# A quarter of the gate section of `w_mod` is loaded early into 16 partitions

## The chip, the cores and the metric

The kernel runs on one core of one Trainium2 chip. The metric is the device time of one execution in microseconds (us). Engines are named as in the profile: PE (TensorE matmul), PEld (TensorE weight load), DVE (VectorE), ACT (ScalarE), POOL (GpSimd), SP (SyncE, which here only issues DMAs). "bufA", "bufB" and "bufC" appear in the profile as bA, bB and bC.

## The reference

One decode step of a block with adaptive layer norm: batch 4, one token each, width 512; attention with 32 heads over a cache of 4096 keys and values of width 128, then a gated MLP. All tensors are bfloat16.

```python
mod = (silu(c) @ w_mod).reshape(4, 6, 1, 512)      # sa, ca, ga, sb, cb, gb
h = layernorm(x) * (1 + ca) + sa
q = h @ wq                                          # 512 -> 32 heads x 128
p = softmax(q @ k_cache^T * 128**-0.5)              # 4 x 32 x 4096 keys
x = x + ga * ((p @ v_cache) @ wo)
h = layernorm(x) * (1 + cb) + sb
z = gelu(h @ w_in); z1, z2 = z[:, :896], layernorm(z[:, 896:])
x = x + gb * ((z1 * (w_sp * z2 + b_sp)) @ w_out)
```

The caches are 2 x 134 MB; everything else together is about 15 MB. `w_mod` has 512 rows of 6 x 512 columns; its last 512 columns make `gb`, the gate of the second half. This is the "gate section", 512 KB.

## The kernel before

Three buffers of 64 KB per partition hold what is loaded. Keys alternate between bufA and bufB, values go to bufC. A "pair" is one load of 8 MB: eight heads of one batch row, 64 KB in each of 128 partitions. `load_k(i)` and `load_v(i)` issue the loads; the loop `for i in range(NT)` has 32 steps of four heads: the first 30 are halves of 15 pairs, the last two (N0 and L) have loads of their own of 4 MB.

All big loads are issued by SP, in program order, so they form one stream: `wq` (4 MB) and the first five sections of `w_mod` (2.5 MB) into bufC, the first key pair in two halves (`load_k(0)`, two issues of L143), the second key pair (`load_k(2)`, L143), and then in the loop values and keys in turn. SP waits for the buffer's last reader before it issues a load into it. ACT issues four tiny loads: `c` and `x` at the very beginning, `w_sp` and `b_sp` (L347, L348) after the queries. The schedule is manual: each engine runs its instructions in the order in which the source records them, and an engine that waits holds up all that stands behind it.

The beginning, in the source's order: `c` is turned by four transposes (`rows_to_cols`), goes through the sigmoid into `cT`, and `mod_rows(0, 2)` (L273) multiplies it with two sections of `w_mod` as rows; ACT copies them to `mrows` (L278), and `mod_turn(2)` (L283) transposes them back to columns. Then come the queries (L323 to L341), `mod_rows(2, 3)` for three more sections, and the loop. In step 0, after the two multiplications of keys (L381) and the first reduction on PE (L389), `late_mod_b` turns the three sections into `modT`, and broadcasts `w_sp` and `b_sp` by a matmul (L356). The first value load may only be issued when all of this has been read, since it overwrites bufC.

In a step, DVE multiplies keys by the query (L381), PE sums over the width with an identity matmul (L389), DVE sums the rest (L401, L412), ACT takes exponentials (L455), and PE multiplies with the values (L510).

The end: `load_end` (called in step L) issues `wo`'s last part (L591, two loads), `w_in` (L594, two), `w_out` (L596, two) and the gate section as `wg_sb` (L601) in four loads of 128 KB, one for each of the four rows that a partition holds. After the last values the chain runs through the projection (L671), the layer norm, the MLP (L836), its normalisation (L220 with `inv_f`), the output product `y` (L862), and `gb` from `wg_sb` and `cT` (L870, 16 matmuls, four for each of the four loads). DVE combines `y` (L890 to L901), multiplies with `gb` (L902), PE transposes (L904), DVE adds `x` (L906) and SP stores (L907).

Of the kernel before, what the change touches and what calls it, by code (L numbers as in the profile page):

```python
# [8 lines left out]
BF16 = mybir.dt.bfloat16  # L9
F32 = mybir.dt.float32  # L10
# [8 lines left out]
RD = 8  # L19
TAIL = (64, 32, 16, 16)  # L20
KIN = (slice(0, 2), slice(2, 4))
KG = tuple(slice(k, k + 1) for k in range(4))
JW = (slice(0, 4), slice(4, 7))
RW = (slice(0, 4), slice(4, 8))

# [26 lines left out]
def kernel(  # L52
# [16 lines left out]
    nc = tc.nc  # L69
    P = 128  # L70
    B, _, D = A_x.shape
    _, H, SK, DH = A_k_cache.shape
    F = B_w_in.shape[1]
    FH = F // 2
    DJ = D // P
# [4 lines left out]
    R = P // HQ  # L80
# [15 lines left out]
    ident_bf = front.tile([P, P], BF16, name="ident_bf")  # L96
# [27 lines left out]
    wm = w_mod.rearrange("(p j) n -> p j n", p=P)  # L124
# [21 lines left out]
    def load_k(i):  # L146
        if i < N0:
            load(bufs[i // 2 % 2], kv_view(A_k_cache, i), (NJ, NJ) if i == 0 else (NP,))
        else:
            load(kts[i], kv_view(A_k_cache, i), (NJ,))  # L150
# [5 lines left out]
            load(vts[i], kv_view(A_v_cache, i), TAIL if i == L else (NJ,))  # L156

    load_k(0)
    load_k(2)

    make_identity(nc, ident_bf)
    ident_f = consts.tile([P, P], F32, name="ident_f")
# [16 lines left out]
    def spread(n, pattern, axis, **sizes):  # L179
# [18 lines left out]
        out=far, in0=half, scalar1=-1.0, scalar2=-NEG, op0=ALU.add, op1=ALU.mult  # L198
# [1 line left out]
    nc.gpsimd.tensor_scalar(  # L200
        out=fars, in0=far[:, :, None].to_broadcast([P, 2, R // 2]), scalar1=-1.0, scalar2=None, op0=ALU.mult
    )
    cT = consts.tile([P, DJ, B], BF16, name="cT")
    pbd8 = consts.tile([P, NP, HP], BF16, name="pbd")
    nc.gpsimd.memset(pbd8, 0.0)
    pbds = pbd8.rearrange("p n q -> p (n q)").rearrange("p (k n q) -> p k n q", k=4, q=HQ)
# [5 lines left out]
    def rows_to_cols(src):  # L212
        t = ps_sm([P, DJ, B], BF16)
        for j in range(DJ):
            nc.tensor.transpose(t[:, j, :], src[0:B, j:D:DJ], ident_bf[0:B, 0:B])
        return t
# [34 lines left out]
        rsqrt(rs, v, 1.0, eps)  # L251
        return xc, rs

    cps = rows_to_cols(c_sb)
    cx = pre.tile([P, DJ, B], F32, name="cx")
    nc.vector.tensor_copy(out=cx, in_=cps)
    sg = pre.tile([P, DJ, B], F32, name="sg")
    nc.vector.tensor_scalar(
        out=sg, in0=cx, scalar1=-60.0, scalar2=-1.0, op0=ALU.max, op1=ALU.mult
    )  # L260
# [19 lines left out]
    def mod_turn(n):  # L280
        mps = ps_sm([P, DJ, n * R])
        for j in range(DJ):
            nc.tensor.transpose(mps[:, j, :], mrows[0:n * R, j:D:DJ], ident_f[0:n * R, 0:n * R])  # L283
        return mps.rearrange("p j (s r) -> p s j r", s=n)[:, :, :, 0:B]
# [6 lines left out]
    nc.vector.tensor_tensor(out=xn, in0=xc1, in1=bc(rs1, DJ), op=ALU.mult)  # L291
    mod_rows(0, 2)
    modA = mod_turn(2)
    hs = pre.tile([P, DJ, B], F32, name="hs")
    nc.vector.scalar_tensor_tensor(  # L295
        out=hs, in0=modA[:, 1], scalar=1.0, in1=xn, op0=ALU.add, op1=ALU.mult
# [49 lines left out]
    sp_t = pre.tile([1, 2], BF16, name="sp_t")  # L346
    nc.scalar.dma_start(out=sp_t[:, 0:1], in_=B_w_sp[0:1, 0:1])  # L347
    nc.scalar.dma_start(out=sp_t[:, 1:2], in_=B_b_sp.rearrange("(a b) -> a b", b=1))  # L348
    modT = consts.tile([P, 3 * DJ, B], F32, name="modT")
    g8 = consts.tile([P, 2, B], F32, name="g8")  # L350
    spf = consts.tile([P, 2], F32, name="spf")

    def late_mod_b():
        mps = mod_turn(3)
        sps = ps_sm([P, 2])
        nc.tensor.matmul(sps, lhsT=ones_b, rhs=sp_t, start=True, stop=True)  # L356
        nc.vector.tensor_copy(
            out=modT.rearrange("p (s j) b -> p s j b", s=3),
            in_=mps,
        )  # L360
        nc.vector.tensor_copy(out=spf, in_=sps)
        nc.gpsimd.tensor_copy(out=g8[:, 1, :], in_=spf[:, 0:1].to_broadcast([P, B]))
        cbT = modT[:, 2 * DJ:3 * DJ, :]
        nc.gpsimd.tensor_scalar_add(out=cbT, in0=cbT, scalar1=1.0)
# [210 lines left out]
    wol_sb = Arena(bufC, 0, 8 * KB).tile([P, HP, D], BF16)  # L575
    win_sb = Arena(bufC, 8 * KB, 22 * KB).tile([P, DJ, F], BF16)
    wout_sb = Arena(bufC, 22 * KB, 29 * KB).tile([P, NH, D], BF16)
    wg_sb = Arena(bufC, 29 * KB, 33 * KB).tile([P, DJ, D], BF16)
    tl = Arena(bufC, 33 * KB, 64 * KB)
    NL = GP * HP * DH  # L580

# [6 lines left out]
    def load_end():  # L588
        wol = A_wo[NL:H * DH].rearrange("(p r) n -> p r n", p=P)
        for rs in RW:  # L590
            nc.sync.dma_start(out=wol_sb[:, rs], in_=wol[:, rs])  # L591
        win = B_w_in.rearrange("(p j) n -> p j n", p=P)
        for ks in KIN:
            nc.sync.dma_start(out=win_sb[:, ks], in_=win[:, ks])  # L594
        for js in JW:
            nc.sync.dma_start(  # L596
                out=wout_sb[:, js],
                in_=B_w_out[js.start * P:js.stop * P].rearrange("(p j) n -> p j n", p=P),
            )
        for ks in KG:  # L600
            nc.sync.dma_start(out=wg_sb[:, ks], in_=wm[:, ks, 5 * D:])  # L601

    acc = late.tile([P, DJ, B], F32, name="acc")
    st2 = late.tile([P, 2, B, DJ + 1], F32, name="st2")
# [75 lines left out]
    for i in range(NT):  # L680
        mult(i, 0)
        if i >= 1:
            scores(i - 1)
        for k in normed_in(i - 1):
            norm_b(k)
        pick = i - 3 if i % 2 == 0 and i >= 4 else None
        if i % 2 and 3 <= i < L:
            pv(i - 2)
        if i % 2 and i < N0:
            load_v(i)  # L690
        reduce_d(i, 0)
        if pick:
            o_pick(pick)
            o_cols(pick)
        if i == L - 1:
            deal(0)
        if i == L:
            deal(2)
            pv(N0 - 1)
            load_end()  # L700
            nc.gpsimd.memset(pbd8, 0.0)  # L701
            nc.vector.memset(opss[1], 0.0)
            exps(N0)
        mult(i, 1)
        if i == 0:
            late_mod_b()
        for k in normed_in(i):
            norm_r(k)
        if pick:
            o_scale(pick)  # L710
        sum8(i, 0)
        if i == L - 1:
            dealt(0)
        if i == L:
            dealt(1)
            dealt(2)
            o_pick(N0 - 1)
            nc.vector.memset(opss[0], 0.0)
        reduce_d(i, 1)
        sum_rest(i)  # L720
        for k in normed_in(i):
            norm_a(k)
        if i == L - 1:
            deal(1)
        if i == L:
            o_cols(N0 - 1)
            project()
        if i % 2 and i + 3 < N0:
            load_k(i + 3)
        elif i == N0 - 3:  # L730
            load_k(N0)
            load_k(L)
        elif i == N0 - 1:
            load_wo()
            load_v(N0)
            late_consts()
        elif i == N0:
            load_v(L)
# [89 lines left out]
    def gate(h, part):  # L828
# [26 lines left out]
        out=zz.rearrange("p f g b -> p g b f"), in0=z1[:, None].to_broadcast([P, 2, B, NH]),  # L855
        in1=st3[:, 0:2], op=ALU.mult,
    )
    y = ps_q()[:, 0:DJ * 2 * B].rearrange("p (j g b) -> p j g b", j=DJ, g=2)
    for js in JW:
        for j in range(DJ):  # L860
# [3 lines left out]
                    start=(j == 0 and f == 0), stop=(f == NH - 1), skip_group_check=True,  # L864
                )

    gb = ps_sm([P, DJ, B])
    for k in range(DJ):
        for j in range(DJ):
            nc.tensor.matmul(  # L870
                gb[:, j, :], lhsT=wg_sb[:, k, j * P:(j + 1) * P], rhs=cT[:, k, :],
                start=(k == 0 and j == 0), stop=(k == DJ - 1), skip_group_check=True,
            )
    mq3 = tl.tile([P, 2, B], F32, name="mq3")
    nc.vector.tensor_reduce(
# [62 lines left out]
```

## Time and profile before

| what | value |
|---|---|
| time, median of 3 runs (lowest to highest) | 663.47 us (663.47 to 663.57) |
| profiled execution: time, span of the core | 663.53 us, 661.7 us |
| mean granted TensorE clock | 0.747 |
| busy share of PE, DVE, ACT, POOL | 48%, 86%, 26%, 3% |
| moved from HBM, mean rate | 282.73 MB, 427 GB/s over the span |
| chain that ended last, by engine | DMA 70%, PE 14%, DVE 10%, ACT 4% |

The profile shows one execution. "Span" runs from the first to the last instruction on the core. The 40 digits of a slice row are busy shares in tenths over equal slices of the span. In a row of the timeline stand the start in us, the busy time in us, the engine, the line of the kernel, the operation, its tiles and sizes, the count, and in brackets the idle time before it and what ended it. Rows with SPq are issues of DMAs by SP's queue. In the waits, the three numbers are the total in us, the count and the longest.

### The profile page before, as it was taken

To read this page: it belongs to the slowest core of one execution; us is meant where nothing else is said; L and a number is where in the kernel's file an instruction comes from. 1 tells how busy PE (TensorE), PEld (TensorE's weight loads), DVE (VectorE), ACT (ScalarE), POOL (GpSimd) and SP (SyncE) were. 2 spreads that over 40 slices of the span, in tenths; PEclk is the share of its full clock that TensorE was granted. 3 is DMA by queue.
4 is the path that set the end of the run, shared out by engine and by line. 5 is a ranking of instruction groups with operands and counts; after the bars stand their busy time and mean duration, and the time that the engine had idled before them with its cause. 6 is when DMAs were issued, how large, how long until landed. Compare 5 with 4: busy or idle time off the path is not lost.

```text
span 661.7 us, 5060 instructions
## 1 busy us (share of the span) xinstructions
PE 316.3 (48%) x2064; PEld 134.6 (20%) x2064; DVE 570.8 (86%) x368; ACT 172.0 (26%) x284; POOL 19.4 (3%) x56
## 2 busy tenths in 40 slices
PE   1565363635154463514446351444535254453885
PEld 0122121212021121202112120111212022121444
DVE  3239999999898998989899898979979898999943
ACT  1220505033060603206060330605023060503322
POOL 3000000000000000000000000000000000030100
PEclk9998787867678785767878576787856778775975
DMA  8999999999999999999999999999999999999996
GB/s 364 447 427 444 440 441 440 441 405 436 440 433 440 444 433 412 445 432 432 437 440 437 424 436 428 433 440 440 429 432 433 428 440 441 420 422 451 414 417 280
DMA packets 8060, 283.07 MB, mean 428 GB/s; under 512 B 860, under 2 KB 1380, under 8 KB 2916
## 3 DMA queue, kind: packets, MB, share of 16 engines
q1 hardware_dynamic: 8016, 282.73, 99.0%
q8 instruction: 16, 0.26, 0.1%
q14 instruction: 8, 0.07, 0.0%
q10 hardware_dynamic: 20, 0.01, 0.0%
HBM read 282.73 MB, written 0.00 MB: 427 GB/s over the span
## 4 chain that ended last, share of the span: by engine, by line
DMA 70%; PE 14%; DVE 10%; ACT 4%; issue 1%; POOL 0%; SPq 0%; ACTq 0%; DVEq 0%
DMA bC<-in_A_v_cache_dram 54%; PE ops L510 11%; DMA bA<-in_A_k_cache_dram 6%; DMA bC<-in_A_wo_dram 4%; DVE S L401 4%; DMA bC<-in_w_mod_dram 4%; DVE bA L381 3%; ACT pbd L455 3%; PE red L389 2%; DMA bC<-in_B_b_sp_dram 2%; DVE bB L381 1%; DVE S L412 1%; PE qps L331 1%; PE sm L323 1%; ACT qbp L341 0%
## 5 line engine op out<-in xcount | busy, mean ns | idle before, releaser
L455 ACT ACTIVATE pbd<-S,nb 32x256 bf16<-32x256 f32 x120 | 154.3, 1520 | 422.6 <-DVE nb L442 421.3
L381 DVE TENSOR_TENSOR bA<-bA,qbp 128x8192 bf16<-128x8192 bf16 x32 | 142.4, 4451 | 21.7 <-DMA bA<-in_A_k_cache_dram 21.7
L389 PE MATMUL red<-bB,ident_bf 128*128 128x512 bf16 x344 | 97.2, 441 | 113.6 <-DVE bB L381 113.6
L389 PE MATMUL red<-bA,ident_bf 128*128 128x512 bf16 x332 | 93.3, 440 | 110.2 <-DVE bA L381 110.2
L389 PEld LDWEIGHTS <-ident_bf 128*128 128x128 bf16 x676 | 72.8, 110 | 337.7 <-issue 175.5
L381 DVE TENSOR_TENSOR bB<-bB,qbp 128x8192 bf16<-128x8192 bf16 x28 | 123.7, 4418 | 13.4 <-DMA bB<-in_A_k_cache_dram 13.4
L510 PE MATMUL ops<-bC,pbd 128*32 128x512 bf16 x960 | 83.6, 525 | 69.9 <-DMA bC<-in_A_v_cache_dram 64.8
L401 DVE TENSOR_REDUCE S<-bA 128x48 f32<-128x6144 bf16 x15 | 98.1, 6543 | 0.0
L401 DVE TENSOR_REDUCE S<-bB 128x48 f32<-128x6144 bf16 x14 | 91.6, 6542 | 0.0
L510 PEld LDWEIGHTS <-pbd 128*32 128x32 bf16 (+1 forms) x1016 | 37.4, 126 | 120.5 <-issue 63.9
L455 ACT ACTIVATION_READ_ACCUMULATOR pbd<-S,nb 32x1 f32 x120 | 58.8, 490 | 0.0
L412 DVE TENSOR_REDUCE S<-red 128x64 f32<-128x512 f32 x64 | 43.7, 683 | 4.4 <-PE red L389 4.3
L469 POOL TENSOR_TENSOR rsb<-maskd,rs 128x8 f32<-128x8 f32 x15 | 3.8, 253 | 556.9 <-ACT pbd L455 556.9
L381 DVE TENSOR_TENSOR bB<-bB,qbo 128x8192 bf16<-128x8192 bf16 x4 | 17.6, 4410 | 0.0
L522 DVE TENSOR_REDUCE osb<-ops 128x128 f32<-128x512 f32 x17 | 11.8, 692 | 0.6
L519 DVE TENSOR_TENSOR ops<-ops,m 128x512 f32<-128x512 f32 x15 | 10.4, 693 | 0.0
L295 DVE SCALAR_TENSOR_TENSOR bC<-sm,bC 128x16 f32<-128x16 f32 x1 | 0.2, 175 | 11.4 <-PE sm L283 11.4
L488 PE MATMUL sm<-rsb,inv_d 128*128 128x32 f32 (+2 forms) x12 | 2.9, 338 | 14.6 <-POOL rsb L469 14.6
L273 PE MATMUL sm<-bC,cT 128*4 128x512 bf16 x20 | 3.7, 621 | 8.4 <-DMA bC<-in_w_mod_dram 8.4
L455 ACT ACTIVATE pbd<-S,nM 32x128 bf16<-32x128 f32 x8 | 4.6, 576 | 12.1 <-POOL pbd L701 10.9
L425 DVE TENSOR_REDUCE mrow<-S 128x1 f32<-128x256 f32 (+1 forms) x17 | 6.9, 404 | 0.6
L331 PE MATMUL qps<-bC 128*128 128x256 bf16 (+1 forms) x16 | 4.5, 383 | 4.1 <-ACT qbp L341 2.8
(159 smaller groups left out, 134.0 us busy)
## 6 DMA issues: line engine op xcount, KB each, us to landing
bA<-in_A_k_cache_dram SPq DMA_DIRECT2D x2, 4096.0 KB, 31.4
bB<-in_A_k_cache_dram SPq DMA_DIRECT2D x2, 4096.0 KB, 41.6
bC<-in_A_wq_dram SPq DMA_DIRECT2D x1, 4096.0 KB, 12.3
bA<-in_A_v_cache_dram SPq DMA_DIRECT2D x1, 4096.0 KB
bA<-in_A_wo_dram SPq DMA_DIRECT2D x1, 3072.0 KB
bC<-in_w_mod_dram SPq DMA_DIRECT2D x1, 2560.0 KB, 18.0
bB<-in_A_v_cache_dram SPq DMA_DIRECT2D x1, 2048.0 KB, 32.3
bC<-in_B_w_in_dram SPq DMA_DIRECT2D x2, 896.0 KB
```

Of the source, the lines that this page charges most:

```text
L323: nc.tensor.matmul(qr[R * q:R * (q + 1)], lhsT=hT[:, k, :], rhs=wq_v[:, k, gs, q, :], start=(k == 0), stop=(k == DJ - 1), tile_position=(0 ...
L331: nc.tensor.matmul(qp[:, 0:npair], lhsT=eb2[k][:, b].rearrange("p k q r -> p (k q r)"), rhs=qrow[:, h, k:2 * npair:2], start=(k == 0), sto ...
L381: nc.vector.tensor_tensor(out=kt, in0=kt, in1=bc(q, KC), op=ALU.mult)
L389: nc.tensor.matmul(red, lhsT=ident_bf, rhs=kt[:, :, m * rd:(m + 1) * rd], start=(m == 0), stop=(m == DH // rd - 1),)
L401: nc.vector.tensor_reduce(out=st[i, "S"][:, n0:NJ], in_=kts[i][:, n0:NJ, :], axis=AX.X, op=ALU.add)
L412: nc.vector.tensor_reduce(out=st[i, "S"][:, kc * KC:kc * KC + on_pe(i, kc)], in_=st.pop((i, "red", kc)), axis=AX.X, op=ALU.add,)
L425: nc.vector.tensor_reduce(out=mrow, in_=S, axis=AX.X, op=ALU.max)
L455: nc.scalar.activation(out=pbd8[r, :, 2 * q + h] if pair(i) else pbds[r, i % 4, :, q], in_=S[r, :], func=AF.Exp, bias=nM[r, h:h + 1], scal ...
L469: nc.gpsimd.tensor_tensor(out=st["P", g, "rsb"][:, b], in0=maskd[:, :, None].to_broadcast([P, HQ, 2]), in1=rs[:, None, :].to_broadcast([P, ...
L510: nc.tensor.matmul(ops_of(i)[g:g + rows], lhsT=pb[:, n, :], rhs=vt[:, n, :], start=(m < 4), stop=(m >= end - 4), tile_position=(0, g),)
L519: nc.vector.tensor_tensor(out=ops, in0=ops, in1=sel[:, :, None].to_broadcast([P, G, DH]), op=ALU.mult)
L522: nc.vector.tensor_reduce(out=osb, in_=ops.rearrange("p g d -> p d g"), axis=AX.X, op=ALU.add)
```

## The change

The gate section is split by its rows. Rows 0 to 383 (`KE` = 3 for each partition) are loaded at the end into `wg_sb` as before, in three loads instead of four. Rows 384 to 511, 128 KB, are loaded early into 16 partitions (`PU`) of the part of `wm_sb` whose two sections `mod_rows(0, 2)` has read: eight rows of 1 KB for each partition, by nine transfers of four partitions (eight of four rows, the last of them cut in two). These nine issues stand in SP's order behind `mod_turn(2)`, and `load_k(2)`, which stood right behind `load_k(0)`, is moved behind them.

`cT` gets 15 groups of columns instead of 4, for the two ways in which `c` is now cut. A new function `mod_uneven` multiplies the early part in rows (eight matmuls over 16 partitions) into rows 96 to 99 of `mrows`; it stands in step 0 just ahead of `late_mod_b`, which now turns four sections instead of three. At the end an identity matmul in float32 brings the early part from `modT` into the accumulator of `gb`, ahead of the product `y`, and twelve matmuls instead of 16 add the rest.

```diff
+KE = 3
+RU = 8
+EV = 128 * KE
+PU = 16
+KU = [[(slice(0, 4),)] * 2 for _ in range(3)] + [[(slice(0, 4),), (slice(0, 2), slice(2, 4))]]
-KG = tuple(slice(k, k + 1) for k in range(4))
+KG = tuple(slice(k, k + 1) for k in range(KE))
...
     load_k(0)
-    load_k(2)
...
-    cT = consts.tile([P, DJ, B], BF16, name="cT")
+    NC = DJ + KE + RU
+    cT = consts.tile([P, NC, B], BF16, name="cT")
...
-    cps = rows_to_cols(c_sb)
-    cx = pre.tile([P, DJ, B], F32, name="cx")
-    nc.vector.tensor_copy(out=cx, in_=cps)
-    sg = pre.tile([P, DJ, B], F32, name="sg")
+    cps = ps_sm([P, NC, B], BF16)
+    cuts = [slice(j, D, DJ) for j in range(DJ)]
+    cuts += [slice(k, EV, KE) for k in range(KE)] + [slice(EV + r, D, RU) for r in range(RU)]
+    for n, cut in enumerate(cuts):
+        pn = P if n < DJ + KE else PU
+        nc.tensor.transpose(cps[0:pn, n, :], c_sb[0:B, cut], ident_bf[0:B, 0:B])
+    cx = pre.tile([P, NC, B], F32, name="cx")
+    nc.gpsimd.memset(cx[:, DJ + KE:], 0.0)
+    nc.vector.tensor_copy(out=cx[:, 0:DJ + KE], in_=cps[:, 0:DJ + KE])
+    nc.vector.tensor_copy(out=cx[0:PU, DJ + KE:], in_=cps[0:PU, DJ + KE:])
+    sg = pre.tile([P, NC, B], F32, name="sg")
...
     mod_rows(0, 2)
     modA = mod_turn(2)
+    wu = w_mod[EV:D, 5 * D:].rearrange("(p s k) n -> p s k n", s=2, k=DJ)
+    for b in range(4):
+        for s in range(2):
+            for ks in KU[b][s]:
+                nc.sync.dma_start(out=wm_sb[b:PU:4, ks, s * D:(s + 1) * D], in_=wu[b:PU:4, s, ks])
+    load_k(2)
...
+    def mod_uneven():
+        mp = ps_sm([P, D])
+        for r in range(RU):
+            nc.tensor.matmul(
+                mp[3 * R:3 * R + B], lhsT=cT[0:PU, DJ + KE + r, :], rhs=wm_sb[0:PU, r % DJ, r // DJ * D:(r // DJ + 1) * D],
+                start=(r == 0), stop=(r == RU - 1), tile_position=(0, 3 * R),
+            )
+        nc.scalar.copy(
+            out=mrows[3 * R:3 * R + B].rearrange("b (p j) -> b j p", j=DJ),
+            in_=mp[3 * R:3 * R + B].rearrange("b (j p) -> b j p", j=DJ),
+        )
...
-        mps = mod_turn(3)
+        mps = mod_turn(4)
...
+        wge = w_mod[0:EV, 5 * D:].rearrange("(p k) n -> p k n", p=P)
         for ks in KG:
-            nc.sync.dma_start(out=wg_sb[:, ks], in_=wm[:, ks, 5 * D:])
+            nc.sync.dma_start(out=wg_sb[:, ks], in_=wge[:, ks])
...
         if i == 0:
+            mod_uneven()
             late_mod_b()
...
+    gb = ps_sm([P, DJ, B])
+    nc.tensor.matmul(
+        gb.rearrange("p j b -> p (j b)"), lhsT=ident_f, rhs=modT[:, 3 * DJ:4 * DJ, :].rearrange("p j b -> p (j b)"),
+        start=True, stop=False, skip_group_check=True,
+    )
     y = ps_q()[:, 0:DJ * 2 * B].rearrange("p (j g b) -> p j g b", j=DJ, g=2)
...
-    gb = ps_sm([P, DJ, B])
-    for k in range(DJ):
+    for k in range(KE):
         for j in range(DJ):
             nc.tensor.matmul(
-                gb[:, j, :], lhsT=wg_sb[:, k, j * P:(j + 1) * P], rhs=cT[:, k, :],
-                start=(k == 0 and j == 0), stop=(k == DJ - 1), skip_group_check=True,
+                gb[:, j, :], lhsT=wg_sb[:, k, j * P:(j + 1) * P], rhs=cT[:, DJ + k, :],
+                start=False, stop=(k == KE - 1), skip_group_check=True,
             )
```

More of the change, by code (lines that the diff above doesn't have):

```diff
@@ L348 @@
     nc.scalar.dma_start(out=sp_t[:, 1:2], in_=B_b_sp.rearrange("(a b) -> a b", b=1))
-    modT = consts.tile([P, 3 * DJ, B], F32, name="modT")
+    modT = consts.tile([P, 4 * DJ, B], F32, name="modT")
     g8 = consts.tile([P, 2, B], F32, name="g8")
     spf = consts.tile([P, 2], F32, name="spf")
+    def mod_uneven():
[9 more added lines that the diff above has]
+        )
     def late_mod_b():
-        mps = mod_turn(3)
+        mps = mod_turn(4)
         sps = ps_sm([P, 2])
@@ L357, in late_mod_b @@
         nc.vector.tensor_copy(
-            out=modT.rearrange("p (s j) b -> p s j b", s=3),
+            out=modT.rearrange("p (s j) b -> p s j b", s=4),
             in_=mps,
@@ L577 @@
     wout_sb = Arena(bufC, 22 * KB, 29 * KB).tile([P, NH, D], BF16)
-    wg_sb = Arena(bufC, 29 * KB, 33 * KB).tile([P, DJ, D], BF16)
+    wg_sb = Arena(bufC, 29 * KB, 33 * KB).tile([P, KE, D], BF16)
     tl = Arena(bufC, 33 * KB, 64 * KB)
```

## The prediction

> **What bounds the kernel now.** I read the page first (engines, queues), then the chain, SP's waits, the timeline at both ends and the windows of the last 10 us. Busy shares, slices, queue:
>
> ```profile
> PE 316.3 (48%) x2064; PEld 134.6 (20%) x2064; DVE 570.8 (86%) x368; ACT 172.0 (26%) x284; POOL 19.4 (3%) x56
> ...
> DMA  8999999999999999999999999999999999999996
> ...
> q1 hardware_dynamic: 8016, 282.73, 99.0%
> ```
>
> SP's queue (q1) keeps the 16 DMA engines busy for 99.0% of the span, at 9 tenths or more in all but the first and last slice. DVE, at 86%, loses its time to that stream: in the groups, L381 waits 21.7 us and 13.4 us for `A_k_cache`. So a hole in the stream lengthens the run by the hole, if nothing behind it was idle anyway. I followed the stream packet by packet in the trace: from 36.5 us to the tail no engine has a gap over 0.1 us. Hence the question: does the change open one?
>
> SP's own waits:
>
> ```profile
> SPq L143 <- PE ops L510: 85.2, 14, 10.4
> SPq L594 <- DMA bA<-in_A_v_cache_dram: 9.3, 1, 9.3
> SPq L601 <- DMA bC<-in_A_wo_dram: 1.8, 2, 0.9
> SPq L601 <- DMA bB<-in_A_v_cache_dram: 1.7, 2, 0.8
> ```
>
> L601 loads `wg` into bufC, yet waits for landings of V in bufB. That is no hazard of data: there are eight landing semaphores, taken in turn by SP's and ACT's loads together, and a load waits until the one eight places before it has landed. The four L601 issues start at 646.64, 647.88, 649.18 and 650.42; the loads eight places before landed at 646.58, 647.82, 649.12 and 650.35. So SP reissues 0.06 us after a landing.
>
> The beginning (timeline):
>
> ```profile
> 1.89 1.36 SPq L143 DMA_DIRECT2D bA<-in_A_k_cache_dram  x2
> 3.29 0.48 SPq L143 DMA_DIRECT2D bB<-in_A_k_cache_dram  x1
> 28.94 8.76 DVE L381 TENSOR_TENSOR bA<-bA,qbp 128x8192 bf16<-128x8192 bf16 x2 [5.24 <-DMA bA<-in_A_k_cache_dram]
> 48.01 0.16 PE L356 MATMUL sm<-bC 1*128 1x2 bf16 x1 [5.12 <-DMA bC<-in_B_b_sp_dram]
> 48.30 0.33 SPq L143 DMA_DIRECT2D bC<-in_A_v_cache_dram  x1
> ```
>
> The second key pair (the bB line) is issued at 3.29, some 34 us before its engines need it. The two halves of the first pair land at 28.85 and 38.58; their last packets end between 37.75 and 38.24, and each engine's next packet follows within 0.01 us.
>
> The end (timeline):
>
> ```profile
> 657.53 0.19 DVE L890 TENSOR_TENSOR bC<-g,qps 128x32 f32<-128x32 f32 x1 [0.18 <-PE qps L862]
> 657.94 0.51 PEld L870 LDWEIGHTS <-bC 128*128 128x128 bf16 x8 [0.21 <-DMA bC<-in_w_mod_dram]
> 658.24 0.17 DVE L901 TENSOR_TENSOR bC<-bC 128x16 f32<-128x16 f32 x1
> 658.58 0.17 DVE L902 TENSOR_TENSOR bC<-bC,sm 128x16 f32<-128x16 f32 x1 [0.16 <-PE sm L870]
> ```
>
> Two paths meet at L902: the last `wg` slice (landed 658.23), and the chain from V's last piece (landed 647.82) to L901's end, 658.41. They differ by 0.2 us. Both hang on the stream.
>
> **The change, part by part**, against the profiled execution: 663.53 us, of which 661.7 is span and 1.8 lies around it; that is 0.06 over the median of 663.47.
>
> *Tail, one slice of four removed.* The slices land at 657.16, 657.50, 657.90 and 658.23, so the last one comes 0.33 earlier, and L902 then waits for L901 alone: 658.58 becomes 658.44, a gain of 0.14.
>
> *Tail, the identity matmul added ahead of L862.* It is a float32 128x16 product in two passes, a form that takes 0.61 us at 639.02 (L220). Here PE finishes L220 and is ready for L862, whose input comes at 656.56 and which starts at 656.61. Bounds: 0 if it fits under that wait, 0.61 if nothing overlaps. L862's first weight load began at 656.22, 0.26 after L220's; an extra pair in between pushes it by as much. I take 0.26. L890 waits for L862, so L901 ends at 658.67. With the slice gone, L902 starts at 658.70: the tail as a whole gets **0.12 longer**.
>
> *Early PE and ACT work.* `mod_uneven` is 8 matmuls of 0.23 (L273: 1.87 for 8), one copy of 0.59 (L278) and 0.66 of transposes: 3.1 us from 42.1, when PE is done with L389, to about 45.3. PE and DVE idle there until 48.0 for the tiny `b_sp` load (the L356 row), so it costs nothing; without that cover it would cost DVE's early work 2.4 us, which still waits on nothing that feeds the stream before 57. The eleven more transposes of `c` (0.07 each) and the wider sigmoid stand before 8 us; their result is wanted at 19.2, when `w_mod` has landed: nothing.
>
> *128 KB on few engines.* Each small transfer has four partitions. `c`, also four partitions, shows four packets of 1,024 B, 0.044 us each, and four landing marks. So I put 32 packets, 1.4 us, on each of four engines. The 16 marks of the last `wg` slice are five near 655.0, three from 655.7 to 656.8 and eight from 657.7 to 658.2. Followed from `c` and `x`, the four engines are among the early ones, so their 1.4 us stays within 2 to 3 us of room: nothing. If they were late ones, V's last piece and the end would come 1.4 later.
>
> *SP's order.* This decides. The nine small issues and then `load_k(2)` are moved behind `mod_turn(2)`. In the built order of the changed kernel the first waits for PE's L283 transposes (23.2 us now), harmless alone: 14 us of the first pair are still to come. But the eight semaphores run out. They are taken by c, wq, x, w_mod, first half, second half, small 1, small 2; then small 3 to 6 wait for c, wq, x, w_mod (landed by 19.2), small 7 for the first half (28.85), **small 8 for the second half (38.58)**, small 9 for small 1, and the second key pair for small 2. SP runs in order, so the second key pair can't be issued before small 8 and 9, after the stream in front of it has drained.
> - 38.58 + 0.06: small 8 issues at 38.64. An issue takes 0.26 (ACT's `x`) to 0.33 (SP's L601), and the next follows 0.05 later: small 9 at about 39.0, the key pair at about 39.35. Small 1 and 2 land before that (their packets follow the first pair's by 0.4 us), so they add no wait.
> - Issue to first packet on idle engines: 0.95 (`c`: 0.73 to 1.68), 1.03 and more (`wq`: 0.73 to 1.76, most engines by 2.07). So packets begin at 40.3 to 40.7, against 37.75 to 38.24 for the old ends: a hole of **2.5** by the middles, 2.05 at the shortest (38.24 to 40.3).
> - At the start the first 32 KB packets took 1.23 to 2.18 instead of 1.21, as if data flowed only from 2.55. If that repeats, data flows 1.8 after issue and the hole is 3.2; if not, 2.5. No row tells which, so I take the middle, **2.8**, and 2.05 and 3.2 as ends.
>
> The Trainium skill (DMA: Bandwidth & Descriptors, "Latency and other measured facts") gives about 0.6 us to the first byte on this kind of queue. By it the hole would be some 0.4 smaller and the sum 666.0. The `c` and `wq` rows of this trace, 0.95 and 1.03, speak for more.
>
> Is the hole filled later? DVE starts 2.5 us earlier (`b_sp` now meets an idle engine), but later loads are already issued 7 to 15 us ahead of need (V at 88.97, while keys still land until 98), so the stream is full again at once and can't catch up.
>
> Sum: 663.53 + 2.8 + 0.12 − 0.06 = **666.4 us**.
>
> **The rivals.**
> 1. *The issue isn't held, or its cover holds:* the second pair's packets follow directly. For it: the issue has a lead of 34 us now. Against: the order of semaphores above and the L601 rows. What is left is the tail: 663.6.
> 2. *Faster: DVE's earlier start reaches the end.* DVE idles from 43.1 to 48.2 for `b_sp`; behind an emptied queue that load lands by about 41, and DVE starts some 2.5 earlier. If DVE and not the stream set the pace, the end would come at 663.5 − 2.5 = 661.0. It decides once DVE stops waiting for keys; against it stand its 35 us of waits for `A_k_cache`.
> 3. *A longer restart:* small issues at 0.55 each (as ACT's first) and the full start-up delay put data at 41.6, a hole of 3.7; with 0.61 for the identity matmul, 667.7.
>
> **How the numbers follow.** Forecast 0.80 (its own range: 663.47 + 2.05 − 0.14 = 665.4, where the identity matmul fits under its cover, to 663.47 + 3.2 + 0.47 = 667.1, where it costs all of 0.61), longer restart 0.09, not held 0.08, faster 0.03. The range 665.3 to 667.8 takes in the first two, which are 0.89. A measurement of this kernel can tell about 0.2%, 1.3 us. Faster: rival 2, 0.03. Same: rival 1, and 0.01 of the forecast for a hole under 1.3, 0.09. Slower: 0.88.
>
> **What would show it.** In the profile after: SP's waits show the small loads' line held by `A_k_cache` until 38.6 us; the second key pair is issued at about 39.4; DMA share near zero around 39 to 40; the `b_sp` wait of 5 us before its matmul gone; V's last piece, L902 and the end all some 2.8 later. I am wrong if the second pair is issued before 37, or if the hole is there and V's last piece still lands at 647.8.

## The result: 674.8 us, slower by 1.7%, and the profile after

The changed kernel takes 674.84 us (median of 6 runs, 673.42 to 675.40) against 663.59 us: a ratio of 1.0166, interval 1.0152 to 1.0180. The prediction said slower, but by 2.9 us; it is 11.3. The profiled execution took 675.02 us with a span of 673.2. One of the six runs of the kernel before took 988.43 us; it stands in the median of 663.59, which it hardly moves, and not in the ratio, which is of fast runs alone.

The page after: engines, DMA share by slices, rate by slices (a slice is now 16.8 us), SP's queue.

```profile
PE 318.3 (47%) x2081; PEld 134.8 (20%) x2081; DVE 569.7 (85%) x369; ACT 173.2 (26%) x285; POOL 19.5 (3%) x57
...
DMA  8987999999999999999999999999999999999996
GB/s 368 442 350 312 436 436 387 433 429 436 429 436 436 436 433 428 432 433 436 437 433 429 436 436 433 437 436 436 437 424 429 428 436 433 437 416 450 414 413 256
...
q1 hardware_dynamic: 8036, 282.73, 97.7%
```

The engines are as busy as before in microseconds, and the same 282.73 MB are moved. What changed is SP's queue: 97.7% of a longer span instead of 99.0%. The rate falls in the third, fourth and seventh slice (350, 312 and 387 GB/s), that is between 34 and 67 us and once more after 101. So there is not one hole but two, and a small third one.

Timeline of the beginning, kernel after (start, busy time, engine, line, operation, tiles, sizes; in brackets the idle time before and what ended it). L310 are the small loads, L148 the keys and values, L313 makes `hs`, L411 multiplies keys, L374 and L378 are `mod_uneven`, L295 is `mod_turn`, L386 the matmul with `w_sp` and `b_sp`:

```profile
22.99 16.54 SPq L310 DMA_DIRECT2D bC<-in_w_mod_dram  x9
39.57 0.44 SPq L148 DMA_DIRECT2D bB<-in_A_k_cache_dram  x1
41.19 0.17 DVE L313 SCALAR_TENSOR_TENSOR bC<-sm,bC 128x16 f32<-128x16 f32 x1 [29.39 <-DMA bC<-in_w_mod_dram]
...
45.31 8.76 DVE L411 TENSOR_TENSOR bA<-bA,qbp 128x8192 bf16<-128x8192 bf16 x2 [3.67 <-ACT qbp L359]
...
60.38 1.88 PE L374 MATMUL sm<-bC,cT 16*4 16x512 bf16 x8
62.30 1.05 ACT L378 COPY bC<-sm 4x512 f32<-4x512 f32 x1 [4.40 <-PE sm L374]
...
63.40 0.75 PE L295 MATMUL sm<-ident_f,bC 128*128 128x128 f32 x4 [1.14 <-ACT bC L378]
...
64.08 0.17 PE L386 MATMUL sm<-bC 1*128 1x2 bf16 x1
...
64.39 0.33 SPq L148 DMA_DIRECT2D bC<-in_A_v_cache_dram  x1
```

SP's wait for the first key pair's landings, kernel after:

```profile
SPq L310 <- DMA bA<-in_A_k_cache_dram: 10.5, 2, 9.0
```

The row that makes `hs`, kernel before:

```profile
23.25 0.17 DVE L295 SCALAR_TENSOR_TENSOR bC<-sm,bC 128x16 f32<-128x16 f32 x1 [11.37 <-PE sm L283]
```

The small loads are held by the landings of the first key pair, as forecast, and the second key pair is issued at 39.57 (39.35 in the forecast). The row of L313 is what the prediction missed: DVE makes `hs` at 41.19 instead of 23.25, and what ended its 29 us of idleness is a load from `w_mod`, one of the small ones. Everything that hangs on `hs` moves with it: the queries, the first multiplication of keys (45.31 instead of 28.94), and the first value load, 64.39 instead of 48.30. By then the second key pair's data had all arrived.

The windows around both holes (width; busy time and instructions of PE, PEld, DVE, ACT, POOL; granted clock; DMA share; GB/s; a packet's bytes count in the window in which it starts):

```profile
36.00:40.00 4.00, 0.00 (x0) 0.00 (x0) 0.00 (x0) 0.00 (x0) 0.00 (x0) 1.00 0.40 162
...
60.00:64.00 4.00, 2.86 (x15) 1.12 (x12) 0.00 (x0) 1.05 (x1) 0.00 (x0) 1.00 0.00 0
```

In 60 to 64 us no packet of more than 4 bytes starts. Added up from the packet records, the 16 DMA engines idle 2.69 us in the mean near 40, 4.84 near 62 and 0.49 near 104 (before: 0.35 up to 600 us, nearly all of it at the start). Moreover the first 64 KB packets behind each hole take 2.5 to 3.4 us instead of 2.42; over the whole run what the 64 KB packets take beyond 2.418 us adds up to 2.81 us per engine instead of 0.48, and 1.6 of it lies right behind the three holes.

The end moved as a block. From the first matmul of the last group with V (647.99 before, 659.43 after) to the product with `gb` (658.58 before, 670.08 after) it is 10.65 us instead of 10.59. Kernel after:

```profile
659.43 0.57 PE L574 MATMUL qps<-pbd,bB 128*128 128x4 bf16 x16
...
667.75 0.57 PE L891 MATMUL sm<-modT,ident_f 128*128 128x16 f32 x2
...
669.09 0.19 DVE L926 TENSOR_TENSOR bC<-g,qps 128x32 f32<-128x32 f32 x1 [0.41 <-PE qps L899]
...
670.08 0.17 DVE L938 TENSOR_TENSOR bC<-bC,sm 128x16 f32<-128x16 f32 x1
```

### The profile page after: what moved, and what is told of

Its sections match the earlier page's. It is cut to its first block, busy times and chain, and to the rows that moved or that the text cites. A ratio compares the mean times of both kernels' runs of the same rounds, so it can differ in the third digit from the quotient of the medians.

```text
span 673.2 us, 5114 instructions
## 1 busy us (share of the span) xinstructions
PE 318.3 (47%) x2081; PEld 134.8 (20%) x2081; DVE 569.7 (85%) x369; ACT 173.2 (26%) x285; POOL 19.5 (3%) x57
## 3 DMA queue, kind: packets, MB, share of 16 engines
q1 hardware_dynamic: 8036, 282.73, 97.7%
HBM read 282.73 MB, written 0.00 MB: 420 GB/s over the span
## 4 chain that ended last, share of the span: by engine, by line
DMA 57%; DVE 26%; PE 13%; ACT 2%; issue 1%; SPq 0%; DVEq 0%; ACTq 0%
DMA bC<-in_A_v_cache_dram 34%; DMA bA<-in_A_k_cache_dram 18%; DVE S L431 10%; DVE bA L411 9%; PE ops L540 7%; DMA bB<-in_A_v_cache_dram 4%; DVE bB L411 4%; PE red L419 3%; DVE S L442 2%; ACT pbd L485 2%; PE qps L349 1%; PE sm L341 1%; DVE osb L552 1%; DVE ops L549 0%; ACT qbp L359 0%
## 5 line engine op out<-in xcount | busy, mean ns | idle before, releaser
L411 DVE TENSOR_TENSOR bA<-bA,qbp 128x8192 bf16<-128x8192 bf16 x32 | 142.4, 4453 | 17.9 <-DMA bA<-in_A_k_cache_dram 14.2
L419 PE MATMUL red<-bA,ident_bf 128*128 128x512 bf16 x332 | 94.9, 445 | 109.5 <-DVE bA L411 109.5
L411 DVE TENSOR_TENSOR bB<-bB,qbp 128x8192 bf16<-128x8192 bf16 x28 | 123.7, 4418 | 12.7 <-DMA bB<-in_A_k_cache_dram 12.7
L540 PE MATMUL ops<-bC,pbd 128*32 128x512 bf16 x960 | 82.2, 518 | 65.1 <-DMA bC<-in_A_v_cache_dram 52.4
L313 DVE SCALAR_TENSOR_TENSOR bC<-sm,bC 128x16 f32<-128x16 f32 x1 | 0.2, 175 | 29.4 <-DMA bC<-in_w_mod_dram 29.4
L411 DVE TENSOR_TENSOR bB<-bB,qbo 128x8192 bf16<-128x8192 bf16 x4 | 17.6, 4411 | 0.0
L341 PE MATMUL sm<-bC 128*32 128x512 bf16 x32 | 3.8, 627 | 18.8 <-DVE bC L318 18.8
L552 DVE TENSOR_REDUCE osb<-ops 128x128 f32<-128x512 f32 x17 | 11.8, 692 | 0.6
```

Of the source, the lines that this page charges most:

```text
L341: nc.tensor.matmul(qr[R * q:R * (q + 1)], lhsT=hT[:, k, :], rhs=wq_v[:, k, gs, q, :], start=(k == 0), stop=(k == DJ - 1), tile_position=(0 ...
L411: nc.vector.tensor_tensor(out=kt, in0=kt, in1=bc(q, KC), op=ALU.mult)
L419: nc.tensor.matmul(red, lhsT=ident_bf, rhs=kt[:, :, m * rd:(m + 1) * rd], start=(m == 0), stop=(m == DH // rd - 1),)
L540: nc.tensor.matmul(ops_of(i)[g:g + rows], lhsT=pb[:, n, :], rhs=vt[:, n, :], start=(m < 4), stop=(m >= end - 4), tile_position=(0, g),)
L552: nc.vector.tensor_reduce(out=osb, in_=ops.rearrange("p g d -> p d g"), axis=AX.X, op=ALU.add)
```

## The experiments

"Idle" and "longer packets" are the two sums named above: mean idle time of a DMA engine, and what its 64 KB packets took beyond 2.418 us each. The last five columns come from one profiled execution of each kernel. The medians of before that belong to the ratios are 663.57 to 663.66 us.

| kernel | us | ratio, interval | `hs` starts | 2nd keys issued | 1st values issued | idle to 600 us | longer packets |
|---|---|---|---|---|---|---|---|
| before | 663.59 | | 23.25 | 3.29 | 48.30 | 0.35 | 0.48 |
| after | 674.84 | 1.0166, 1.0152 to 1.0180 | 41.19 | 39.57 | 64.39 | 8.35 | 2.81 |
| e_contig9 | 669.00 | 1.0080, 1.0066 to 1.0094 | 23.58 | 41.33 | 46.78 | 4.26 | 1.29 |
| e_strided8 | 674.47 | 1.0162, 1.0148 to 1.0176 | 40.21 | 26.30 | 63.63 | 7.69 | 2.30 |
| e_contig8 | 665.49 | 1.0028, 1.0017 to 1.0038 | 23.50 | 29.10 | 50.41 | 0.32 | 1.42 |
| e_two16 | 665.15 | 1.0022, 1.0014 to 1.0031 | 23.46 | 22.15 | 49.78 | 0.36 | 1.28 |
| e_own_strided | 664.33 | 1.0011, 1.0002 to 1.0020 | 23.23 | 28.89 | 48.96 | 0.33 | 0.50 |
| e_own_neigh | 664.92 | 1.0019, 1.0011 to 1.0028 | 23.34 | 28.97 | 49.73 | 0.31 | 0.99 |
| e_own_first | 664.31 | 1.0010, 1.0001 to 1.0019 | 23.59 | 13.09 | 48.79 | 0.36 | 0.48 |
| e_own_nine | 667.89 | 1.0065, 1.0050 to 1.0080 | 23.23 | 39.92 | 45.69 | 3.20 | 1.45 |
| e_dve_late | 668.57 | 1.0075, 1.0062 to 1.0089 | 38.72 | 3.21 | 58.50 | 3.19 | 2.32 |
| e_own_late | 671.91 | 1.0121, 1.0104 to 1.0138 | 38.71 | 13.78 | 61.54 | 6.11 | 1.80 |
| e_two16_early | 665.12 | 1.0022, 1.0012 to 1.0031 | 23.24 | 21.93 | 49.71 | 0.30 | 1.28 |
| e_own_best | 664.23 | 1.0008, 0.9999 to 1.0017 | 23.56 | 29.25 | 48.90 | 0.35 | 0.54 |

### Which partitions, and how many loads

Why does DVE wait for the small loads? `hs` lies at another place of bufC than `wm_sb` and shares no byte with it. In the program, though, DVE waits ahead of L313 for the landing semaphores of all nine small loads. The theory (A): when the program's waits are put in, a load into every fourth partition is taken to overlap with what it doesn't touch, and one into neighbouring partitions isn't. Four kernels change only the slices of the small loads.

```diff
# e_contig9: nine loads, neighbouring partitions
-wm_sb[b:PU:4, ks, ...], in_=wu[b:PU:4, s, ks]
+wm_sb[4 * b:4 * b + 4, ks, ...], in_=wu[4 * b:4 * b + 4, s, ks]
# e_strided8: four loads of eight partitions, every second one
+for b in range(2): ... wm_sb[b:PU:2, :, ...], in_=wu[b:PU:2, s]
# e_contig8: four loads of eight neighbouring partitions
+for b in range(2): ... wm_sb[8 * b:8 * b + 8, :, ...], in_=wu[8 * b:8 * b + 8, s]
# e_two16: two loads of sixteen partitions
+wm_sb[0:PU, :, s * D:(s + 1) * D], in_=wu[:, s]
```

**e_contig9.**

> All of the change stays; each of the nine small loads writes four neighbouring partitions (4b to 4b+3) instead of every fourth (b, b+4, ...). Theory A (two causes: the eight landing semaphores hold the second key pair, and, apart from that, DVE's L313 is made to wait for the small loads because their strided partitions are taken to overlap its output in bufC): L313 starts at about 23.3 us again, the value load is issued before 57, and only the hole ahead of the second key pair is left. Here that pair stands behind the landing of the second half, three more small issues of 0.66 and the tiny loads, so it is issued at 41 to 42: a hole of about 4, and 668 to 670 us. Theory B (the late second key pair alone makes all of it, DVE's wait follows from it): L313 stays at 41, and the time at about 675.

**e_strided8.**

> All of the change stays; the 128 KB come in four loads of eight partitions each, every second one (b, b+2, ...). Theory A: semaphores suffice, so the second key pair is issued at about 26 us and follows without a hole; but L312 (L313 of the change) still waits for the small loads until about 39, the queries and the first key product come 16 us later, the first value load is issued at about 62 instead of 48.3, and the stream has a hole of 5 to 6 there: 669 to 672 us. Theory B: no hole, 663.6.

**e_contig8.**

> As the run before, but the four loads write eight neighbouring partitions each (8b to 8b+7). Theory A: neither wait is left, the second key pair is issued at about 28.6, the stream has no hole, and the time is 663.5 to 663.9 us (the tail of the prediction, +0.12, and up to 0.3 if late DMA engines carry some of the 128 KB). Theory B: 663.6 as well; this run tells whether anything else of the change costs time.

**e_two16.**

> As the run before, with two loads of 16 neighbouring partitions, so that all 16 DMA engines take 8 KB each ahead of the values. Theory A: no hole; V's last piece lands up to 0.35 later than in the run before, since the late engines carry their share again: 663.7 to 664.1. If the choice of engines does not matter: the same as the run before to 0.1.

Timeline of e_contig9: nine loads still hold the second key pair, but DVE starts on time.

```profile
21.41 19.88 SPq L310 DMA_DIRECT2D bC<-in_w_mod_dram  x9
...
23.58 0.18 DVE L313 SCALAR_TENSOR_TENSOR bC<-sm,bC 128x16 f32<-128x16 f32 x1 [11.55 <-PE sm L295]
...
41.33 0.36 SPq L148 DMA_DIRECT2D bB<-in_A_k_cache_dram  x1
```

Timeline of e_strided8: four loads let the key pair go at 26.30, but DVE waits for a landing behind the first pair.

```profile
26.30 0.44 SPq L148 DMA_DIRECT2D bB<-in_A_k_cache_dram  x1
40.21 0.17 DVE L312 SCALAR_TENSOR_TENSOR bC<-sm,bC 128x16 f32<-128x16 f32 x1 [28.22 <-DMA bC<-in_w_mod_dram]
...
63.63 0.33 SPq L148 DMA_DIRECT2D bC<-in_A_v_cache_dram  x1
```

Timeline of e_contig8: neither wait is left.

```profile
23.50 0.17 DVE L312 SCALAR_TENSOR_TENSOR bC<-sm,bC 128x16 f32<-128x16 f32 x1 [11.50 <-PE sm L295]
29.10 0.36 SPq L148 DMA_DIRECT2D bB<-in_A_k_cache_dram  x1
...
50.41 0.35 SPq L148 DMA_DIRECT2D bC<-in_A_v_cache_dram  x1
```

The two causes come apart. At four loads the choice of partitions alone makes 674.47 − 665.49 = 9.0 us; at neighbouring partitions the step from four to nine loads makes 669.00 − 665.49 = 3.5. Either cause is enough for a hole, and the prediction had only the second. SP is made to wait as well: with strided partitions the first small load is issued at 22.99, behind the transposes of `mod_turn(2)`, and with neighbouring ones at 21.41 (e_contig9), ahead of them. That the choice of partitions puts these waits in is shown; that it does so through a test of overlap that is too coarse for strided partitions is the theory that fits, and no run tests it by itself.

e_contig9 came out as expected. e_strided8 lies 2.5 us over its 669 to 672: its holes add up to 7.4 us instead of 5 to 6, and the longer packets come on top. e_contig8 and e_two16, without either, missed their expected 663.5 to 664.1 by 1 to 2 us: no hole is left there (0.32 and 0.36 us, as before), yet the first 64 KB packets behind the small ones take 2.6 to 3.7 us instead of 2.42.

### A place of its own

The next kernels put the early part into `pbd`'s tile (4 KB in 32 partitions, four rows each, empty until the exponentials), which shares no buffer with `hs`, so no overlap with `hs` can be assumed. In e_own_strided the partitions are still every fourth one. `mod_uneven` then has four matmuls over 32 partitions instead of eight over 16, and the clearing of the tile moves from the beginning to behind `mod_uneven`. e_own_first loads it in one piece ahead of the first key pair, with the identity matmul away from the tail.

```diff
# e_own_strided
+wu_sb = pbd8[0:PU]...            # PU = 32, RU = 4
+for b in range(4): dma_start(out=wu_sb[b:PU:4], in_=wu[b:PU:4])
# e_own_first
+dma_start(out=wu_sb, in_=wu)     # ahead of load_k(0); load_k(2) back right behind it
```

**e_own_strided.**

> The early part goes into another tile (pbd's, 4 KB in each of 32 partitions, empty until step N0's preparation) by four loads of eight partitions each, again every fourth partition (b, b+4, ...). It shares no buffer with wm_sb, hs or hT. A, the overlap theory (the time is lost because DVE's L311 is made to wait for the small loads, and the first value load with it): L311 starts near 23.5 us as with neighbouring partitions, the second key pair is issued before 30, the first value load near 50, no hole near 60 to 68, and the time is that of four loads of neighbouring partitions, 665.0 to 665.8. B, every fourth partition costs by itself (slower landings or slower large loads behind them): the first value load or the packets stay late, and the time stays near 674.

**e_own_first.**

> The early part goes into pbd's tile by one load of 32 neighbouring partitions, issued ahead of the first key pair; the second key pair's load stands in its old place, right behind load_k(0); the identity matmul stands ahead of the gate of the attention, away from the tail. A, the large packets behind the small ones take longer, 0.9 us in all: 664.4 to 664.8. B, that cost belongs to small loads that come into a full stream behind the key pair, and ahead of the first key pair there is none: 663.6 to 664.1 (128 KB more ahead of V's last piece is 0.3 us, one slice less in the tail gives some 0.1 to 0.3 back). Neither gives a time under 663.2.

Timeline of e_own_strided:

```profile
23.23 0.17 DVE L311 SCALAR_TENSOR_TENSOR bC<-sm,bC 128x16 f32<-128x16 f32 x1 [11.42 <-PE sm L296]
...
28.89 0.34 SPq L148 DMA_DIRECT2D bB<-in_A_k_cache_dram  x1
...
48.96 0.33 SPq L148 DMA_DIRECT2D bC<-in_A_v_cache_dram  x1
```

664.33 us: loads into every fourth partition cost nothing by themselves; what cost 9 us was the wait. It came out 0.7 below theory A's range, and that is a finding of its own: the 128 small packets run at the same place in the stream as in e_contig8 (from 37.7 us on), each takes 46 ns, and the 64 KB packets behind them take 2.42 us. So "small packets ahead" isn't what slows large ones, as I had expected of both kernels. e_own_first, 664.31, fell between its two theories: the first 32 KB packets of the first key pair, right behind the small ones, take 1.37 to 1.55 us there instead of 1.21, once, and that is 0.25 us.

### Neighbouring partitions

e_own_neigh differs from e_own_strided in one thing: which eight partitions a load takes.

```diff
-dma_start(out=wu_sb[b:PU:4], in_=wu[b:PU:4])
+dma_start(out=wu_sb[8 * b:8 * b + 8], in_=wu[8 * b:8 * b + 8])
```

> As e_own_strided, but each of the four loads takes eight neighbouring partitions (8b to 8b+7) instead of every fourth one. Tile, sizes, order and waits are the same. A, what slows the stream is several DMA engines writing to neighbouring partitions at once (the SBUF page's rule that four neighbouring partitions share a port): the small packets take longer than 46 ns in the mean, the second pair's first 64 KB packets about 3.2 to 3.6 us instead of 2.42 on all engines, some 0.9 us in all as with e_contig8: 664.9 to 665.4. B, it was bufC as the target and not the partitions: packets of 46 ns and 2.42 us, and e_own_strided's time, 664.3.

664.92 against 664.33 us, with intervals of the ratio that overlap (1.0011 to 1.0028, 1.0002 to 1.0020); the trace is clearer than the times. The small packets take 53 ns in the mean and up to 108, and the 16 first packets of the second pair 2.66 to 2.97 us each instead of 2.418: 0.5 us per engine in all, and V's last group starts 0.65 later. Theory A in kind; in size half of the 0.9 that I had put.

### The late DVE alone, the nine loads alone, both with `mod_uneven`

e_dve_late is the kernel before with one 2-byte copy that makes DVE wait for the first pair's second half. e_own_nine keeps the hole of the prediction and takes the late DVE away; for the order of the semaphores its loads of `w_sp` and `b_sp` stand at the beginning. e_own_late is e_own_strided with the late DVE; its second key pair is issued at 13.78 instead of 28.89, and both are well ahead of its turn in the stream.

```diff
# e_dve_late (on before), e_own_late (on e_own_strided)
+lag = pre.tile([P, 1], BF16, name="lag")
+nc.vector.tensor_copy(out=lag, in_=bufA[:, NP - 1, DH - 1:DH])
 hs = pre.tile([P, DJ, B], F32, name="hs")
# e_own_nine (on e_own_strided)
+for b in range(8): ... dma_start(out=wu_sb[b:PU:8, ks], in_=wu[b:PU:8, ks])   # nine in all
+the two loads of w_sp and b_sp right behind x
```

**e_dve_late.**

> The kernel before, with one addition: ahead of the line that makes hs, DVE copies one column of the first key pair's second half into a 2-byte tile, so that it waits for that half (38.6 us). No load is added, moved or changed. A, a late DVE alone opens the hole: the first value load is issued some 23 us after hs, at about 62 instead of 48.3, the second pair's data end at about 57.4, packets begin again at 62.9, a hole of 5.5; with 0.5 near 104 and 1.3 for the slower first packets behind the holes 7.3 in all: 670.9, between 669.8 and 672.0. B, as the prediction put it, the later loads' lead of 7 to 15 us takes up what DVE loses: 663.5 to 664.3.

**e_own_nine.**

> The early part in pbd's tile (32 partitions, no overlap with hs), by nine loads of four partitions, b, b+8, b+16, b+24, and the second key pair's load behind them; the loads of w_sp and b_sp stand at the beginning, so that the eight landing semaphores come round as in the changed kernel: small 8 waits for the second half of the first pair, the key pair for small 2. It keeps the hole that the prediction worked out and takes away the wait that it missed. A, two separate causes: DVE's line of hs starts near 23.5, the key pair is issued at 39.5 to 40.0, a hole of 2.7 and 0.6 for slower first packets behind it: 664.3 + 3.3 = 667.6, between 667.0 and 668.2. The prediction's own sum for this, without the slower first packets, 666.4 to 667.1. B, the ordered small loads are the cause of the second hole as well (the value load stays near 64): 672 and more.

**e_own_late.**

> e_own_strided (the early part in pbd's tile, no hole at the second key pair) with e_dve_late's addition: DVE copies one column of the first pair's second half ahead of hs and so starts at 38.7 us. It tells what mod_uneven's matmuls, its copy and the fourth section to be turned (3.1 to 3.4 us from the trace of the changed kernel: 60.38 to 64.08 there, against 57.44 to 58.19 with a late DVE and no early part) cost once the wait for b_sp no longer covers them. A, they come in full on top of the hole: the first value load is issued at 61.6 to 62.0 instead of e_dve_late's 58.50, and the time is 664.33 + 4.91 (e_dve_late against before) + 3.2 = 672.4, between 671.6 and 673.0. B, they stay covered, as the prediction had it: value load near 58.5, and 664.33 + 4.91 = 669.2.

Timeline of e_dve_late:

```profile
38.72 0.17 DVE L297 SCALAR_TENSOR_TENSOR bC<-sm,bC 128x16 f32<-128x16 f32 x1
...
57.66 0.60 PE L283 MATMUL sm<-ident_f,bC 96*128 96x96 f32 x4
...
58.20 0.17 PE L358 MATMUL sm<-bC 1*128 1x2 bf16 x1
...
58.50 0.33 SPq L143 DMA_DIRECT2D bC<-in_A_v_cache_dram  x1
```

Timeline of e_own_late:

```profile
38.71 0.17 DVE L313 SCALAR_TENSOR_TENSOR bC<-sm,bC 128x16 f32<-128x16 f32 x1
...
58.38 1.02 PE L374 MATMUL sm<-pbd,cT 32*4 32x512 bf16 x4
59.43 1.06 ACT L378 COPY bC<-sm 4x512 f32<-4x512 f32 x1 [4.01 <-PE sm L374]
...
61.23 0.17 PE L386 MATMUL sm<-bC 1*128 1x2 bf16 x1
...
61.54 0.33 SPq L148 DMA_DIRECT2D bC<-in_A_v_cache_dram  x1
```

Without any small load, a late DVE alone makes 4.9 us: theory B, that the loads' lead takes it up, has fallen. It is less than the expected 7.3, because I had taken the 23 us from `hs` to the value load out of the changed kernel's trace, and 3 of them are `mod_uneven`. e_own_late shows just that: with the same start of DVE (38.71), the value load is issued 3.04 us later (61.54 against 58.50), and the time, 671.91, is 2.67 over the sum of the two parts (664.33 + 4.91). The times of e_own_late spread over 1.4 us, so the 2.67 is rough. In the kernel after, where the eight matmuls take 1.88 us instead of 1.02 for four, the value load comes 23.20 us behind `hs`, against 22.83 here and 19.78 in e_dve_late. In the kernel before, PE waited 5.1 us for `b_sp` at this place and would have hidden it; here the packet of `b_sp` starts at 57.82, and PE comes to its matmul only at 61.23.

e_own_nine shows the hole of the prediction alone: DVE on time (23.23), the key pair at 39.92, 667.89 us, that is 3.56 more than e_own_strided, with 2.87 us more of idle and 0.95 of longer packets.

### The tail, and the best version

e_two16_early is e_two16, and e_own_best is e_own_strided, each with the identity matmul moved to before the gate of the attention.

```diff
+gb = ps_sm([P, DJ, B]); the identity matmul     # ahead of gate(1, 0)
 gate(1, 0)
...
-gb = ps_sm([P, DJ, B]); the identity matmul     # ahead of y
```

**e_two16_early.**

> As e_two16 (two loads of 16 neighbouring partitions), but with the identity matmul of the gate section moved from the tail to before the gate of the attention. It tells the size of that term of the prediction (0.26 us, bounds 0 and 0.61). A, the identity matmul costs 0.26 in the tail: from the first matmul of V's last group to the last product with gb 10.5 us instead of e_two16's 10.76, and the time 664.9 against 665.15. B, it costs nothing there: 10.76 and 665.15 again.

**e_own_best.**

> As e_own_strided, with the identity matmul moved out of the tail to before the gate of the attention. What is left against the kernel before is 128 KB on eight engines ahead of V, and one slice less at the end. From the first matmul of V's last group to the last product with gb 10.55 us instead of e_own_strided's 10.80, and the time 664.1 if both runs' tails are alike otherwise, 664.3 if the tail's difference is chance. Faster than before (under 663.3) only if the removed slice of 0.14 us came through whole and the bytes cost nothing.

From the last group with V to the product with `gb`: 10.76 to 10.57 us, and 10.80 to 10.62. One stretch of it shows the cost in all the traces: from the start of the MLP's normalisation matmuls (L220 before, L225 after) to the first one of `y` it is 0.87 to 0.88 us in the nine kernels with the identity matmul in between, and 0.64 to 0.65 in the five without. So the identity matmul takes 0.23 us of the tail; in the times (665.15 to 665.12, 664.33 to 664.23) that can't be told from nothing. e_own_best, with everything known taken away, is the fastest of the versions with an early part: 664.23, ratio 1.0008, interval 0.9999 to 1.0017. It does not beat the kernel before. The removed slice brings nothing that the runs show: from the first matmul of `y` to the product with `gb` it is 1.97 us before and 1.91 to 1.92 in the kernels with three slices, but 1.91 as well in e_dve_late, which has all four.

## Why the prediction was wrong

The direction and the first hole were right, but that hole makes only about 3.5 of the 11.25 us. The step that failed is the one on the early work, together with the sentence that DVE starts earlier: the prediction has no wait of DVE for the small loads, and it lets nothing early hold up the stream before 57 us. The runs show that DVE is 17.9 us late and that the stream stands still a second time, for 4.84 us. Both of the prediction's own signs of being wrong stayed away (second pair before 37, V's last piece still at 647.8): they looked at the first hole only.

1. **The wait that was missed (4.9 us).** The prediction went through the waits of the changed kernel for SP's queue only, and took it for granted that DVE makes `hs` at 23 us. DVE's own waits there name all nine small loads. So "DVE starts 2.5 us earlier" had the wrong sign: `hs` comes 17.9 us later. Shown by e_contig8 against e_strided8 (9.0 us with what follows in point 2), and by e_dve_late, 4.91 us without any small load.
2. **"Early PE and ACT work: it costs nothing" (2.7 us).** The cover was named (the wait for `b_sp`), and the price without it too, but then dismissed: it "waits on nothing that feeds the stream before 57". The first value load does wait for it, and at 57 the second pair's data end. e_own_late against e_dve_late: the value load 3.04 us later, the time 2.67. The size, 3.1 us, was about right; that it is covered was wrong.
3. **"Later loads are already issued 7 to 15 us ahead."** True of the loads at 88.97 and later in the kernel before; in the kernel after the value load of 88.97 is issued at 103.79, and the 0.49 us near 104 follow. The first value load, at 48.30, has a lead too: its packets could begin at 49.3, the second pair's end at 57.1 to 57.6, so 8 us of slack. I never set a possible delay of DVE against that number; 16.1 us of delay, less 8, and less the 3.3 by which the first hole shifts the pair's own end, is 4.8, and the second hole is 4.84.
4. **The hole before the second key pair: right in place, low in its whole cost.** Idle 2.69 against a forecast of 2.8 (2.05 to 3.2). The issue at 39.57 against 39.35: the small issues stood 0.66 apart and not 0.38, from 38.24 instead of 38.64. The forecast took 0.26 to 0.33 for an issue from other loads; into neighbouring partitions the small ones do take 0.25 to 0.32 (e_contig9), into every fourth one 0.62. What I had as the upper end, that data flow slowly at first, comes on top: 0.6 us, so 3.3 in all, and 3.56 in e_own_nine's time. From the start of the issue to the first packet it took 1.09 us, of which the issue itself is 0.44 and the rest 0.65. The Trainium skill gives about 0.6 us to the first byte (DMA: Bandwidth & Descriptors, "Latency and other measured facts"). Counted from the end of the issue, the trace agrees with it; the prediction compared it with a time counted from the start, so its 666.0 does not follow.
5. **The tail: 0.06 longer against 0.12.** The matmul takes 0.23 (forecast 0.26); the slice's 0.14 is not there, at most 0.06, which e_dve_late shows with all four slices. That the net comes near is partly luck: the stretch from V's last group to the normalisation took 7.86 us instead of 7.97, and it lies anywhere up to 8.12 (e_own_nine).
6. **128 KB on four engines: nothing, they said.** In e_own_strided 0.67 us remain over before, with the identity matmul's 0.23 in it; e_own_best leaves 0.57. Its 128 small packets of 46 ns now stand ahead of V, 0.37 us per engine in the mean, and V's last piece lands 0.32 later (648.14 instead of 647.82). So the bytes are not nothing but some 0.3 us; on four engines, as in the kernel after, they were not tried alone.

The parts measured one at a time add up to 0.67 (e_own_strided) + 3.56 (nine loads) + 4.91 (late DVE) + 2.67 (`mod_uneven` uncovered) = 11.8 us, against 11.25 measured. They are not independent: in the kernel after `hs` is 2.5 us later than with the late DVE alone, which adds to the second hole, and the first hole shifts the end of the second pair, which takes from it. So the sum shows that the list is about complete, and not the size of each part there. Of the rivals, "not held" fell with the issue at 39.57. "DVE's earlier start" fell with the start at 41.19. "A longer restart" had its issue interval nearly right (0.55 for 0.66), but 667.7 is about e_own_nine's 667.89: it too knew one hole only.

What stays open: why the first large packets behind a hole are slow even where nothing small is near (0.4 us at 65 in the kernel after). The packet sums, 8.0 us more of idle, 2.3 of longer packets and 0.37 of small packets ahead of V, are 10.7. V's last piece lands in 16 marks, and their mean moved by 10.83 (646.20 to 657.04). The last mark moved by 11.42 (647.82 to 659.24), which is what V's last group (11.44) waits for: the other 0.6 is that the engines end less evenly. Why they do is open as well.

## What to carry to other kernels

Where a load is moved or added, read in the program who waits for it on every engine, not only on the queue that issues it: a load that shares no byte with a tile can still be waited for by the tile's writer. Then give each load that feeds a saturated stream its slack (when the data ahead of it end, less its issue and 1 us) and set every delay of its readers against that; what is covered by a wait stays covered only as long as that wait is there. And where each load waits for the one eight places before it, every small load ahead of a large one moves the large one's wait to a later landing: into neighbouring partitions, two loads of 16 did the same work as nine of four, 3.9 us cheaper (665.15 against 669.00).

## What the runs showed of the hardware

Small packets slowed the large ones around them for some sets of target partitions and not for others. With the early part in the same tile and at the same place in the stream, loads of eight partitions that lie four apart left all packets alone (46 ns, 2.418 us); loads of eight neighbouring partitions slowed the 16 large packets next to them to 2.66 to 2.97 us. In bufC, loads of eight partitions that lie two apart slowed them to 2.64 to 2.94 (e_strided8), and two loads of 16 partitions to 2.64 to 3.42. The Trainium skill (SBUF — State Buffer, "Door 1: The DMA port swizzle") states that four neighbouring partitions share one DMA port, so that the partitions 0 to 15 reach four ports of 16. The order of the runs agrees with it; that a port is the cause was not tried in another way.

A DMA queue that has run dry restarts in two steps. From the start of the issue to the first packet it takes 0.96 to 1.09 us (64.39 to 65.35, 39.57 to 40.66), of which the issue is 0.33 to 0.44. Then the first packets of 64 KB take 2.5 to 3.4 us instead of 2.418, in the mean 0.4 to 0.6 us more.
